# Fewer zero matmuls in front (30 for 43) and six q, k and v loads in flight for four, in a linear-attention and expert-attention kernel

## The chip, the cores and the metric

The kernel runs on one core of one Trainium2 chip. The metric is the device time of one execution in microseconds, lower is better. Three runs of the kernel before are shown.

## The reference

```
kv   = einsum('bhsd,bhse->bhde', k, v)
out  = einsum('bhsd,bhde->bhse', q, kv)
x    = out / sqrt(mean(out^2, -1) + 1e-6) * g_norm   # then heads side by side: (8, 576, 512)
logits = x @ w_gate                                  # top 2 of 4 experts per token, softmax over them
for e in range(4):
    q, k, v = x @ wq[e], x @ wk[e], x @ wv[e]
    a  = causal softmax(q @ k.T / 8)
    ye = a @ v @ wo[e]
    out += weight of e for the token * ye
```

Batch 8, 8 heads, sequence 576, head size 64; four experts with a head of 64 each. q, k and v are float32 in HBM and are read once (9.4 MB each); the result, again 9.4 MB, is written once.

## The kernel before, in words

One core works through eight batches b = 0 to 7. Every piece of work is a task with a name and a batch, and the sequence of all tasks is written out by hand in the string ORDER (lines 30 to 52); `unpack` (line 116) decodes it and the loop at the end of the kernel (lines 840 to 844) emits one task after the other. So each engine executes its instructions in the order in which they come in that string, and a wait at the head of an engine holds everything behind it. The strings ENGINE and SLOTS fix which engine takes a task and which buffer or PSUM bank it uses.

The tasks that the text speaks of:

- `lk`, `lv`, `lq` (lines 332 to 350): loads of half of the k, v or q data of a batch, issued from the SP queue. A batch has four pieces of k, four of v and two of q. k and v have two buffers each.
- `lw` and `ws` (lines 373 to 387): load of half of an expert weight into a stage buffer, and the multiplication by g_norm that puts it into place (on POOL, DVE or ACT).
- `kv` (line 408): for one chunk of two heads, ten matmuls of k with v (line 414). `kvc` and `kvx` copy the result out of PSUM (`kvs`, by ACT or DVE) and, exchanged between groups of 32 partitions, once more (`kvm`, by ACT, DVE or POOL).
- `qc` (line 435): DVE transposes q in blocks (line 437). `o` (line 442) multiplies it with kvs and kvm (line 450).
- `sq`, `ms`, `ln` to `lo`, `bc`, `xm`: squares, sums (line 482), the inverse root, its spreading by matmul (line 563) and the normalised x (line 571, DVE).
- `G` (line 485, the gate's matmuls), `L`, `lt`: the logits of the gate.
- `kp`, `qp`, `v`: projections (lines 643 and 624); `sc`, `exp`, `msk`, `pv`: scores, exponentials, causal mask, weighted sum (lines 674, 686, 693, 719); `y` and `st`: output projection (line 794) and store (line 811).

Batch 0 is split in halves of heads. Its order on the tensor engine is: zero matmuls, `kv` of chunks 2 and 3, zero matmuls, `o` of the second half, zero matmuls, `kv` of chunks 0 and 1, the sums of the second half, zero matmuls, `o` of the first half. On DVE two transposes of q stand ahead of two of the kvm copies that the first `o` reads.

The zero matmuls come from the table ZEROS (line 26): the key is the task ahead of which they stand, the value their number. Each multiplies a 128x128 tile of zeros with itself (line 836) into a part of a bank that the task is about to use and that nothing reads; in float32 each one is two passes, so that 43 of them are 86 passes in the profile. They wait for nothing but the memset of the zeros and whoever holds the bank. No result depends on them.

FLIGHT (line 19) is used in one place:

```
def queued(task, ins):
    if len(task) > 1 and task[0] in ("lk", "lv", "lq") and task[1] > 1:
        tc.add_manual_dep(ins.ins, moved[-FLIGHT].name, order_only, reason="queue")
    moved.append(ins.ins)
```

`moved` is the list of all loads and stores that went through `queued`. A q, k or v load of batch 2 or later waits until the transfer FLIGHT places earlier in that list has landed. Loads of batches 0 and 1, weights and stores carry no such wait. Apart from it, a transfer waits for the semaphore lane that it takes, of which there are eight, and a load for the release of its buffer. The wait stands in the SP queue, so that it also holds what comes behind it there.

Of the kernel before, what the change touches and what calls it, by code (L numbers as in the profile page):

```python
# [15 lines left out]

NB, NCH, EP, NF = 5, 4, 2, 4
RUN, LO = 9, 4
FLIGHT = 4

NQT, BY_PE = 1, (0, 1, 2, 3, 4, 5, 6, 7)

# [1 line left out]


ZEROS = {
    ("kv", 0, 2): 26, ("o", 0, 1): 9, ("kv", 0, 0): 4, ("o", 0, 0): 4,
}

ORDER = (  # L30
# [96 lines left out]
def kernel(  # L127
# [195 lines left out]
# [4 lines that stand above are left out]
# [548 lines left out]
```

## Time and profile before

| | |
|---|---|
| median of 3 runs | 205.02 us (203.74 to 207.45) |
| the profiled execution's own time | 206.06 us |
| its span, first to last instruction | 204.4 us |
| PE busy (matmuls) | 191.1 us, 94% |
| PEld (weight loads) | 155.5 us, 76% |
| DVE, ACT, POOL busy | 135.9, 129.7, 70.6 us |
| read from HBM, written | 30.42 MB, 9.44 MB |

The profile is of one execution. Its times are counted from the first instruction; busy times of matmuls contain modelled ends, and consecutive ones overlap in a row's duration. The chain of work that ended last is followed back from the last instruction; a piece "DMA k_b<-in_k_dram" in it reaches from the issue of a load to its landing. A row of the timeline gives start, duration, engine, line, operation and tiles, and in brackets the idle time before and what ended it.

### The profile page before, as it was taken

Reading aid. Unit: us, or ns where it says so; the run is one execution under the profiler, and the core shown is the slowest. Engines: PE = TensorE matmul, PEld = TensorE weight load, DVE = VectorE, ACT = ScalarE, POOL = GpSimd, SP = SyncE. Lnnn points to the kernel's source line nnn. Section 1 sums busy time; section 2 is a strip of 40 time slices with the busy share of each in tenths; the row PEclk is TensorE's granted clock in tenths of the full one; section 3 lists DMA queues with packets and bytes.
Section 4 is the critical chain, followed back from the end, with each engine's and each line's share of the span. In section 5 each row is a group of like instructions: output and inputs, shape, how many; then the busy total and the mean of one; then the engine's idle time right before and its main releaser. Section 6 shows DMA issues by size and latency. Waiting matters only on the chain.

```text
span 204.4 us, 7128 instructions
## 1 busy us (share of the span) xinstructions
PE 191.1 (94%) x2943; PEld 155.5 (76%) x2960; DVE 135.9 (66%) x336; ACT 129.7 (63%) x240; POOL 70.6 (35%) x185
## 2 busy tenths in 40 slices
PE   7999899999999889999999999999999999999980
PEld 7976575788787568869878697888967878988740
DVE  7046799969446756766695557765877596667640
ACT  2035536749767268963875978887376647567961
POOL 8101354004355131408163552165126224126500
PEclk9999999999999999999999999999999999999999
DMA  4899997898986998785089960100043134026486
GB/s 151 267 363 354 334 226 196 275 343 247 272 275 213 301 291 310 220 281 192 5 238 337 288 236 3 55 3 0 3 154 145 62 114 152 2 89 205 168 326 195
DMA packets 33808, 40.31 MB, mean 197 GB/s; under 512 B 8288, under 2 KB 24944, under 8 KB 33776
## 3 DMA queue, kind: packets, MB, share of 16 engines
q1 hardware_dynamic: 33248, 39.20, 60.6%
q10 hardware_dynamic: 432, 0.66, 0.9%
q8 instruction: 23, 0.38, 0.8%
q14 instruction: 9, 0.07, 0.1%
q0 software_dynamic: 96, 0.01, 0.1%
HBM read 30.42 MB, written 9.44 MB: 195 GB/s over the span
## 4 chain that ended last, share of the span: by engine, by line
PE 63%; DMA 21%; DVE 5%; ACT 5%; issue 3%; ACTq 0%; POOL 0%; DVEq 0%; SPq 0%; POOLq 0%
PE banks L643 10%; PE banks L450 7%; PE banks L674 7%; DMA k_b<-in_k_dram 7%; DMA q_b<-in_q_dram 6%; PE banks L836 6%; PE banks L624 6%; PE banks L414 6%; PE banks L719 6%; PE banks L482 5%; PE banks L794 5%; DMA v_b<-in_v_dram 5%; DMA out_dram<-stage 4%; PE banks L563 2%; PE banks L762 2%
## 5 line engine op out<-in xcount | busy, mean ns | idle before, releaser
L686 ACT ACTIVATE PT<-banks 128x1024 bf16<-128x1024 f32 (+1 forms) x64 | 51.7, 835 | 11.9 <-PE banks L674 10.2
L693 POOL TENSOR_SCALAR_AFFINE_SELECT PT<-PT 128x256 bf16<-128x256 bf16 (+1 forms) x80 | 29.1, 386 | 20.6 <-ACT PT L686 20.3
L437 DVE STREAM_TRANSPOSE qT<-q_b 128x576 f32<-128x576 f32 x32 | 23.7, 758 | 8.5 <-DMA q_b<-in_q_dram 6.2
L571 DVE TENSOR_TENSOR xT<-banks,ob 128x576 fp32r<-128x576 f32 x32 | 23.4, 746 | 4.1 <-PE banks L563 3.8
L624 PE MATMUL banks<-wv_r,xT 128*128 128x256 f32 x160 | 24.5, 291 | 0.0
L643 PE MATMUL banks<-xT,wk_r 128*128 128x288 f32 x128 | 22.3, 307 | 0.1
L624 PEld LDWEIGHTS banks<-wv_r,xT 128*128 128x128 f32 x160 | 21.2, 189 | 1.4 <-DVE wv_r L387 0.2
L643 PE MATMUL banks<-xT,wq_r 128*128 128x288 f32 x128 | 22.1, 305 | 0.1
L414 PE MATMUL banks<-v_b,k_b 128*64 128x64 f32 x640 | 21.3, 224 | 0.9 <-DMA k_b<-in_k_dram 0.5
L414 PEld LDWEIGHTS banks<-v_b,k_b 128*64 128x64 f32 x640 | 19.7, 138 | 3.1 <-issue 0.9
L674 PE MATMUL banks<-qTp,kT 64*128 64x192 f32 (+3 forms) x224 | 21.3, 307 | 0.4 <-DVE xT L571 0.3
L674 PEld LDWEIGHTS banks<-qTp,kT 64*128 64x128 f32 x224 | 15.8, 185 | 6.0 <-issue 2.0
L643 PEld LDWEIGHTS banks<-xT,wk_r 128*128 128x128 f32 x128 | 18.4, 188 | 1.8 <-ACT ob L311 0.5
L643 PEld LDWEIGHTS banks<-xT,wq_r 128*128 128x128 f32 x128 | 18.3, 188 | 1.9 <-DVE kT L312 0.5
L450 PE MATMUL banks<-qT,kvs 32*64 32x288 f32 x256 | 19.0, 410 | 0.4 <-DVE g_den L608 0.3
L719 PEld LDWEIGHTS <-PT 128*128 128x128 bf16 x480 | 15.9, 97 | 4.5 <-issue 1.5
L474 POOL TENSOR_TENSOR sqs<-ob 128x576 f32<-128x576 f32 x14 | 16.1, 1156 | 7.7 <-DVE ob L312 4.9
L719 PE MATMUL banks<-vext,PT 128*128 128x65 bf16 x480 | 17.5, 193 | 1.0 <-issue 1.0
L450 PE MATMUL banks<-qT,kvm 32*64 32x288 f32 x256 | 18.2, 410 | 0.0
L794 PE MATMUL banks<-wo_b,OT 128*128 128x512 bf16 (+1 forms) x57 | 16.5, 372 | 1.8 <-issue 1.0
L311 ACT COPY stage<-banks 128x512 f32<-128x512 f32 x25 | 14.3, 593 | 5.8 <-PE banks L794 3.4
L311 ACT COPY ob<-banks 128x576 f32<-128x576 f32 x19 | 11.8, 637 | 8.2 <-PE banks L450 8.2
(95 smaller groups left out, 305.9 us busy)
## 6 DMA issues: line engine op xcount, KB each, us to landing
q_b<-in_q_dram SPq DMA_DIRECT2D x16, 576.0 KB, 6.2
out_dram<-stage SPq DMA_DIRECT2D x29, 256.0 KB, 2.6
v_b<-in_v_dram SPq DMA_DIRECT2D x16, 320.0 KB, 5.4
k_b<-in_k_dram SPq DMA_DIRECT2D x16, 320.0 KB, 4.8
v_b<-in_v_dram SPq DMA_DIRECT2D x16, 256.0 KB, 5.0
k_b<-in_k_dram SPq DMA_DIRECT2D x16, 256.0 KB, 5.2
out_dram<-stage SPq DMA_DIRECT2D x9, 128.0 KB, 2.4
stage<-in_moe_wk_dram SPq DMA_DIRECT2D x2, 256.0 KB, 7.3
```

What stands on the lines that cost most here:

```text
L311: return nc.scalar.copy(dst, src)
L414: use(nc.tensor.matmul(p_kv[hh * Dh : (hh + 1) * Dh, c, :], lhsT=k_t(b)[:, h, j, :], rhs=v_t(b)[:, h, j, :], start=(j == 0), stop=(j == LO ...
L437: nc.vector.transpose(q_part(b, dh)[:, ms].rearrange("p m (t i) -> p m t i", t=RUN), q_t(b)[:, ms, :, dh * 32 : (dh + 1) * 32],)
L450: use(nc.tensor.matmul(bank(n)[at : at + Dh, 0:HALF], lhsT=(kvs if z == dh else kvm)[b % 2][pp, m], rhs=q_part(b, dh)[pp, m], start=(dh == ...
L571: use(nc.vector.tensor_tensor(out=xTs[b % 2][:, 0 : NCH * S].rearrange("p (n s) -> p n s", s=S)[:, cs, cols], in0=both(ns)[:, :, 0:HALF], ...
L624: use(nc.tensor.matmul(bank(n)[:, at : at + E * Hd], lhsT=blocks_of(xTs[b % 2], c)[:, i * P : (i + 1) * P], rhs=w_r["v"][:, c, :, :].rearr ...
L643: use(nc.tensor.matmul(bank(n)[:, 0:HALF], lhsT=w_r[nm][:, c, 2 * pr : 2 * pr + 2, :].rearrange("p e f -> p (e f)"), rhs=blocks_of(xTs[b % ...
L674: use(nc.tensor.matmul(bank(ns[el])[:, o : o + hi - lo], lhsT=kTs[(2 * b + pr) % 3][pp, kb * P : (kb + 1) * P], rhs=tiles["qTp", b, pr][pp ...
L686: use(nc.scalar.activation(PTs[(2 * b + pr) % 3][:, :, 512 * j : 512 * j + o], both(ns)[:, :, 0:o], ACTF.Exp, scale=scale), *ns)
L693: nc.gpsimd.affine_select(out=d, in_=d, compare_op=AluOpType.is_ge, fill=0.0, base=0, pattern=[[0, 2], [1, w]], channel_multiplier=-1,)
L719: use(nc.tensor.matmul(heads[el][:, k_ * W1 : (k_ + 1) * W1], lhsT=PT[:, el, col : col + P], rhs=vexts[b % 2][:, kb, 2 * pr + el, :], star ...
L794: use(nc.tensor.matmul(bank(n)[:, 0 : cols.stop - cols.start], lhsT=OT[:, pr, at : at + P], rhs=wo_b[:, pr, cols], start=(pr == 0), stop=( ...
```

## The change

Two constants are changed. The four groups of zero matmuls have 20, 6, 2 and 2 members where they had 26, 9, 4 and 4, and FLIGHT is six where it was four.

```
-FLIGHT = 4
+FLIGHT = 6
...
 ZEROS = {
-    ("kv", 0, 2): 26, ("o", 0, 1): 9, ("kv", 0, 0): 4, ("o", 0, 0): 4,
+    ("kv", 0, 2): 20, ("o", 0, 1): 6, ("kv", 0, 0): 2, ("o", 0, 0): 2,
 }
```

Apart from 13 zero matmuls less, the sequence of instructions is the same on all engines and in the SP queue. What differs in the SP queue is which earlier transfer a load waits for.

## The prediction

> **What bounds the kernel now.** I read the page first, then who waited on PE, the chain that ended last, busy time by stretch, and last the single rows of the front.
>
> ```profile
> span 204.4 us, 7128 instructions
> PE 191.1 (94%) x2943; PEld 155.5 (76%) x2960; DVE 135.9 (66%) x336; ACT 129.7 (63%) x240; POOL 70.6 (35%) x185
> ```
>
> ```profile
> PE banks L719 <- issue: 1.0, 1, 1.0
> PE banks L414 <- DMA k_b<-in_k_dram: 0.5, 1, 0.5
> PE banks L414 <- ACT PT L686: 0.4, 1, 0.4
> PE banks L674 <- DVE xT L571: 0.3, 1, 0.3
> ```
>
> PE is busy for 94% of the span and works in a fixed order, so only two things can shorten the run: PE work that goes away, and PE's few waits. (The columns of the second view: us in total, times, longest.) The zeros are PE work that nobody reads. Their place in the chain that ended last, each row with its start and length:
>
> ```profile
> 1.12 8.11 PE banks L836 x52
> 9.23 1.34 PE banks L414 x40
> 10.59 0.28 ACT kvs L311
> 10.91 2.27 PE banks L836 x18
> 13.18 1.16 PE banks L450 x32
> 14.34 1.09 PE banks L836 x8
> 15.43 1.31 PE banks L414 x40
> 16.74 1.09 PE banks L482 x8
> 17.84 1.09 PE banks L836 x8
> 18.93 1.24 PE banks L450 x32
> ```
>
> The second half of the change concerns the loads of batches 2 to 7. The same chain later:
>
> ```profile
> 33.00 4.51 DMA k_b<-in_k_dram
> 37.52 5.19 DMA k_b<-in_k_dram
> ...
> 64.91 3.59 DMA k_b<-in_k_dram
> 68.49 0.14 issue
> 68.63 1.40 PE banks L414 x34
> ```
>
> From 33.00 to 68.49 seven loads follow each other without a gap, each issued as an earlier one lands, and PE's L414 at 68.63 waits for the last. This is the limit of four in flight. Loads in the front, which have no such limit, and loads in the middle (time to landing, shortest, median, longest; after it the DMA share and GB/s, the last two columns, of a stretch of each):
>
> ```profile
> DMA to landing us min/median/max: 7.0/7.7/8.2
> ```
>
> ```profile
> DMA to landing us min/median/max: 3.8/4.8/6.6
> ```
>
> ```profile
> 16.50:23.40 6.90, 5.96 (x84) 3.72 (x80) 4.87 (x12) 4.47 (x10) 0.57 (x2) 1.00 1.12 338
> 43.00:68.60 25.60, 24.03 (x448) 19.96 (x447) 16.52 (x37) 18.06 (x29) 10.07 (x24) 1.00 0.86 267
> ```
>
> A deeper queue makes each load later after its issue (7.7 for 4.8 us) but moves more: 338 for 267 GB/s.
>
> **Part 1, the zeros.** Price of a pass, from the zeros alone (PE busy and count are the first columns after the length):
>
> ```profile
> 1.12:4.97 3.85, 3.85 (x18) 1.00 0.62 188
> 4.97:9.16 4.19, 4.19 (x36) 1.00 0.87 275
> ```
>
> Before 4.97 a pass takes 3.85 / 18 = 0.214 us, after it 4.19 / 34 = 0.123 (two of the 36 began earlier), although the granted clock reads 1.00 in both. The six zeros removed from the first group are 12 passes of the fast kind: 1.48 us, and the first group would end at 9.16 - 1.48 = 7.68. The others: six passes of 2.27 / 18 = 0.126, 0.76 us; twice four of 1.09 / 8 = 0.136, 1.09 us. In all 3.3 us of PE time. What of it arrives depends on what is late next, step by step.
>
> ```profile
> 2.97 0.62 SPq L332 DMA_DIRECT2D k_b<-in_k_dram  x1
> 6.24 1.50 SPq L332 DMA_DIRECT2D k_b<-in_k_dram  x1
> ```
>
> ```profile
> k_b<-in_k_dram SPq DMA_DIRECT2D x1, 256.0 KB, 5.4
> ```
>
> ```profile
> k_b<-in_k_dram SPq DMA_DIRECT2D x1, 256.0 KB, 7.7
> ```
>
> ```profile
> 10.30 1.44 DVE L437 STREAM_TRANSPOSE qT<-q_b 128x576 f32<-128x576 f32 x2 [4.88 <-DMA q_b<-in_q_dram]
> 11.77 0.47 DVE L312 COPY kvm<-kvs 32x128 f32<-32x128 f32 x2
> 15.90 1.44 DVE L437 STREAM_TRANSPOSE qT<-q_b 128x576 f32<-128x576 f32 x2
> 64.91 0.78 DVE L437 STREAM_TRANSPOSE qT<-q_b 128x576 f32<-128x576 f32 x1 [1.31 <-DMA q_b<-in_q_dram]
> ```
>
> The last k piece of the first half lands at 2.97 + 5.4 = 8.4; with the 0.14 us from landing to matmul of the chain's end above, the first kv starts at 8.5: 0.7 earlier, not 1.48. The second group of zeros would end at 11.7; o(0,1) then waits for DVE's kvm copies at 11.77 to 12.24, which stand behind transposes that start with the landing of q: o starts at 12.1 to 12.3, 0.9 earlier. kv(0,0) waits for the k piece that lands at 6.24 + 7.7 = 13.9 and starts at 14.1, 1.3 earlier. The sums follow; then two zeros instead of four, 0.55 less: o(0,0) starts at 17.0, 1.9 earlier. It reads the first of DVE's two transposes at once and the second half way, at 17.6; they are done at 16.6 and 17.34 even if nothing moves them.
>
> From here the gain passes through ACT and DVE. The projections of k wait for a weight that POOL scales:
>
> ```profile
> 23.64 3.19 POOL L387 TENSOR_SCALAR wk_r<-stage,g_part 128x256 fp32r<-128x256 f32 x3 [5.82 <-DMA stage<-in_moe_wk_dram]
> ```
>
> ```profile
> 28.27 1.29 PE L643 MATMUL banks<-xT,wk_r 128*128 128x288 f32 x8
> ```
>
> POOL starts when the weight lands, behind loads that run at full rate, so it ends at 26.83 in both kernels. L643 can't start before 26.9: 1.4 earlier. What follows on DVE waits for neither POOL nor this load, so PE may get a little of the 1.9 back. I take **1.5 us** for this part. Its ends: 0.9 (the gain of the first o, should the sums' chain be held) and 3.3 (all of the zeros' time). I take the value near 1.4 because two landings and the POOL row hold it there.
>
> **Part 2, six in flight.** With 338 for 267 GB/s the stretch from 33.00 to 68.49 would take 35.5 x 267 / 338 = 28.0 us. Six is less deep than the front's queue of up to eight, so the true lead is between nothing and 7.5 us; the front's lead of 1.5 has to be covered, and 2 to 5 us are likely, more than any wait needs. PE then loses the 0.52 us ahead of L414 at 68.63, and the 0.35 ahead of L674: xT stood behind DVE's transpose at 64.91, which waited 1.31 us for q. Of the 0.36 ahead of L414 at 63.49, ACT's exponentials keep most; I count 0.13. Together **1.0 us**; ends 0 (the lead is used up) and 1.2 (all three). No load is put ahead of another in the SP queue, and a load's buffer is still released by PE, now 1.5 us earlier. Behind the load that waits in SP stand other loads and the first two stores; none waits longer than now. Costs: the PE wait of 1.0 at L719 has no data wait behind it and I leave it as it is (rival three).
>
> **Sum.** 1.5 + 1.0 = 2.5 us. Of the profiled execution: 206.06 - 2.5 = 203.6. That execution was 1.04 above the median of the three runs, so on the median: 205.02 - 2.5 = **202.5**, 1.2% faster.
>
> **A rule beside it.** In this trace the pass of the zeros gets short 3.85 us after PE starts. The Trainium skill, "TensorE: Matmul & The Clock Gate", Part 1, says that the tensor clock is doubled only after a busy window of about 3.4 us, and that this window runs freely, so that the same kernel meets it after different numbers of matmuls. By that rule the change would come at 3.4 to 6.8 us of work, the trace's 3.85 being an early draw, and part 1 would be worth more in other executions (rival one). The same page (Why this matters for your kernels) warns of PE idle gaps over about 3 us; the waits that the sum opens in the front are 0.8 us (7.68 to 8.5) and less, so by it nothing is lost; the trace agrees as far as 16.50 to 23.40 goes, 0.94 us idle in 6.90 with passes still short.
>
> **The rivals.** One: the short passes begin later in most executions. If none came inside the zeros, the 12 removed passes cost 12 x 0.214 = 2.6 and the first kv starts that much earlier; all zeros together 4.4 us. With 1.0 of part 2 the bounds are 3.3 + 1.0 and 4.4 + 1.0 (2.6 + 0.76 + 1.09 = 4.4), that is 200.7 to 199.6; I name **200.5**. For it: runs from 203.74 to 207.45 differ by more than the sum. Against: POOL's 26.83 caps the gain as soon as the front is early.
>
> Two: the gain is hidden. The idle time opened in the front slows PE's passes again (18 passes at 0.214 for 0.123: 1.6 us), or the lead is lost at the DVE chain: 0 to -0.9 us, **204.5**. Against: waits of 0.5 us in the front now don't do it.
>
> Three, the other side: PE's instructions come late. The 0.99 us wait at L719 is put to "issue", no landing and no semaphore; PE's program is fetched by the same 16 DMA engines:
>
> ```profile
> q8 instruction: 11, 0.18, 0.8%
> ```
>
> That is the count of 30 to 118 us, where six will be in flight. If each fetch cost PE one such wait: 11 x 0.99 = 10.9 us more, 205.02 - 2.5 + 10.9 = **213.4**. It turns the sum from three such waits on, and it is slower by over 2% from seven. Against: in the front, with more in flight, no PE wait is put to issue. The Trainium skill, "DMA: Bandwidth & Descriptors" (Queues, rings and completion order), says that an engine takes turns between queue rows packet by packet; by it a longer row of loads would hold a fetch no longer than a short one, and no run yet shows it.
>
> **How the numbers follow.** The forecast 0.50, rival one 0.25, two 0.12, three 0.13. Two per cent, 4.1 us, is about what a measurement of this kernel can tell from no change. Rival one lies beyond it on the fast side: faster 0.25. Of rival three 0.11 lies beyond it: slower 0.11; the rest, 0.64, within. The forecast's own range is 200.9 to 204.1 (from the two per cent, where rival one begins, to the parts' lower ends, 0.9 and 0). The range 199.7 to 206.8 takes in rival one, rival two, and rival three up to four waits (202.5 + 4 x 0.99 = 206.5), and leaves out some 0.15.
>
> **What would show it.** In the changed profile the first L414 starts at 8.5, right behind a k landing; L450 at 12.1 to 12.3 and 17.0; L643 at 26.9 behind POOL's wk_r; no L414 waits for DMA near 67; loads take 6 to 7 us to land and 43 to 68 shows over 300 GB/s. It would be wrong if the first L643 starts later than 27.5, if L414 still waits for k_b, or if new PE waits put to issue appear.

## The result and the profile after

The kernel after takes 202.71 us (median of 18 runs, 201.67 to 204.51), the kernel before beside it 205.11 (18 runs, 203.74 to 207.78). The ratio is 0.9913, with a 95% interval from 0.9883 to 0.9942. The profiled execution of after took 203.93 us, its span is 202.2. (Ratios here and below leave out executions that took over 1.5% more than their kernel's fastest; medians have all of them.)

That profiled execution lost part of its clock in the front, and its page shows it. The span, the busy times and the granted clock in 40 slices:

```profile
span 202.2 us, 7076 instructions
PE 188.7 (93%) x2917; PEld 153.2 (76%) x2934; DVE 135.5 (67%) x336; ACT 129.6 (64%) x240; POOL 70.3 (35%) x185
PEclk9969999999999999999999999999999999999996
```

The third slice, 10 to 15 us, has a granted clock of 0.6, all the others but the last 0.9 or more. Who waited on PE, the columns as before:

```profile
PE banks L414 <- DMA k_b<-in_k_dram: 2.5, 1, 2.5
PE banks L563 <- DVE lo L520: 1.3, 2, 1.0
```

One wait for a k piece is left, and it is in the front. The waits at L674 and L719 and the one of L414 near 68 us are gone. The chain of after shows the same:

```profile
2.96 6.80 DMA k_b<-in_k_dram
...
9.90 1.40 PE banks L414 x40
...
11.64 2.93 PE banks L836 x12
14.57 1.21 PE banks L450 x32
15.77 0.64 PE banks L836 x4
16.41 1.31 PE banks L414 x40
...
67.99 1.32 PE banks L414 x40
```

The k piece issued at 2.96 takes 6.8 us to land where it took 5.4 before. PE has finished its zeros by 7.42 and starts the first kv at 9.90. Twelve zero passes then take 2.93 us. The stretches (the columns behind the busy times are granted clock, DMA share and GB/s; in the first two rows the stretch is 3.41 us, one period of the clock, as shown below):

```profile
7.85:11.26 3.41, 1.36 (x40) 1.28 (x40) 0.00 (x0) 0.00 (x0) 0.00 (x0) 1.00 0.95 303
11.26:14.68 3.42, 3.06 (x21) 2.82 (x28) 1.88 (x4) 0.86 (x3) 0.00 (x0) 0.50 1.06 376
...
43.00:67.90 24.90, 24.48 (x454) 20.51 (x454) 16.25 (x38) 17.49 (x29) 9.99 (x24) 1.00 0.94 312
```

PE was idle for 3.41 - 1.36 = 2.05 us of the first stretch, and in the next its clock was 0.50. From 43 to 68 us the loads now move 312 GB/s (267 before).

To compare all kernels I cut PE's time at three points that all of them have: the first matmul of the kv of batch 2, the first L762 (it follows the L719 that waited before), and PE's last matmul. The cuts are starts and ends of PE rows of each trace, in us; the second column is the landing of the last k piece that the first kv needs, which is issued at 2.96 in every kernel.

| profiled kernel | k piece lands | kv of batch 2 starts | from there to L762 | from L762 to PE's end |
|---|---|---|---|---|
| before | 8.37 | 43.38 | 30.97 | 124.56 |
| after | 9.76 | 44.02 | 28.44 | 124.32 |

So in these two executions the front cost 0.64 us more, the middle 2.53 less and the rest 0.24 less; the tail behind PE is 5.44 in both. The sum is 2.13; the spans differ by 2.2 as they are rounded here, by 2.14 unrounded.

### The profile page after: what moved, and what is told of

Same layout as the page of the kernel before. It is cut to its first block, busy times and chain, and to the rows that moved or that the text cites. A ratio compares the mean times of both kernels' runs of the same rounds, so it can differ in the third digit from the quotient of the medians.

```text
span 202.2 us, 7076 instructions
## 1 busy us (share of the span) xinstructions
PE 188.7 (93%) x2917; PEld 153.2 (76%) x2934; DVE 135.5 (67%) x336; ACT 129.6 (64%) x240; POOL 70.3 (35%) x185
## 4 chain that ended last, share of the span: by engine, by line
PE 74%; DVE 8%; ACT 5%; DMA 5%; issue 4%; POOL 1%; SPq 0%; DVEq 0%; ACTq 0%; POOLq 0%
PE banks L643 13%; PE banks L414 9%; PE banks L674 8%; PE banks L450 8%; PE banks L482 8%; PE banks L624 7%; PE banks L719 6%; PE banks L794 6%; DMA k_b<-in_k_dram 3%; PE banks L563 3%; DVE qT L437 3%; PE banks L762 2%; PE banks L836 2%; DMA out_dram<-stage 2%; PE banks L545 1%
## 5 line engine op out<-in xcount | busy, mean ns | idle before, releaser
L414 PE MATMUL banks<-v_b,k_b 128*64 128x64 f32 x640 | 21.1, 224 | 2.5 <-DMA k_b<-in_k_dram 2.5
L414 PEld LDWEIGHTS banks<-v_b,k_b 128*64 128x64 f32 x640 | 19.7, 138 | 4.6 <-issue 3.0
L643 PE MATMUL banks<-xT,wk_r 128*128 128x288 f32 x128 | 22.3, 307 | 0.1
L643 PE MATMUL banks<-xT,wq_r 128*128 128x288 f32 x128 | 22.1, 305 | 0.1
L674 PE MATMUL banks<-qTp,kT 64*128 64x192 f32 (+3 forms) x224 | 21.3, 307 | 0.0
L674 PEld LDWEIGHTS banks<-qTp,kT 64*128 64x128 f32 x224 | 15.8, 185 | 5.5 <-issue 2.0
L643 PEld LDWEIGHTS banks<-xT,wk_r 128*128 128x128 f32 x128 | 18.4, 188 | 1.8 <-ACT ob L311 0.5
L643 PEld LDWEIGHTS banks<-xT,wq_r 128*128 128x128 f32 x128 | 18.2, 188 | 1.9 <-DVE kT L312 0.5
L450 PE MATMUL banks<-qT,kvs 32*64 32x288 f32 x256 | 19.1, 412 | 0.4 <-DVE g_den L608 0.3
L719 PEld LDWEIGHTS <-PT 128*128 128x128 bf16 x480 | 15.8, 97 | 3.4 <-DVE ob L312 0.9
L450 PE MATMUL banks<-qT,kvm 32*64 32x288 f32 x256 | 18.3, 411 | 0.0
L311 ACT COPY stage<-banks 128x512 f32<-128x512 f32 x25 | 14.1, 593 | 5.4 <-PE banks L794 4.1
L719 PE MATMUL banks<-vext,PT 128*128 128x65 bf16 x480 | 17.4, 193 | 0.0
```

The lines of the kernel that those rows point to most:

```text
L311: return nc.scalar.copy(dst, src)
L414: use(nc.tensor.matmul(p_kv[hh * Dh : (hh + 1) * Dh, c, :], lhsT=k_t(b)[:, h, j, :], rhs=v_t(b)[:, h, j, :], start=(j == 0), stop=(j == LO ...
L450: use(nc.tensor.matmul(bank(n)[at : at + Dh, 0:HALF], lhsT=(kvs if z == dh else kvm)[b % 2][pp, m], rhs=q_part(b, dh)[pp, m], start=(dh == ...
L643: use(nc.tensor.matmul(bank(n)[:, 0:HALF], lhsT=w_r[nm][:, c, 2 * pr : 2 * pr + 2, :].rearrange("p e f -> p (e f)"), rhs=blocks_of(xTs[b % ...
L674: use(nc.tensor.matmul(bank(ns[el])[:, o : o + hi - lo], lhsT=kTs[(2 * b + pr) % 3][pp, kb * P : (kb + 1) * P], rhs=tiles["qTp", b, pr][pp ...
L719: use(nc.tensor.matmul(heads[el][:, k_ * W1 : (k_ + 1) * W1], lhsT=PT[:, el, col : col + P], rhs=vexts[b % 2][:, kb, 2 * pr + el, :], star ...
```

## The experiments

The theory after this profile had three parts. The zeros are worth about 1.4 us when the k piece lands as before, and in the profiled execution a late landing and the clock hid that. Six in flight removes the waits for loads near 63 to 69 us. And the wait put to issue at L719 is a packet of PE's instructions that starts late while loads are queued: the theory of the held packet, D where it has a letter. The rivals: the deeper queue alone did it all; the zeros alone did it all; the wait at L719 belongs to its place in the program and has nothing to do with loads.

**One part alone.** The first kernel has the new zeros and four in flight, the second the old zeros and six.

```
 FLIGHT = 4
-    ("kv", 0, 2): 26, ("o", 0, 1): 9, ("kv", 0, 0): 4, ("o", 0, 0): 4,
+    ("kv", 0, 2): 20, ("o", 0, 1): 6, ("kv", 0, 0): 2, ("o", 0, 0): 2,
```

> Theory A (the prediction): fewer zeros are worth 1.5 us by themselves: ratio to the kernel before near 0.993, about 203.6 us, and the first L643 starts near 26.9. Theory B (from the changed kernel's profile, where the first kv waited 2.48 us for a k piece and L643 started 0.6 later than before): the zeros are worth nothing, 0 to +0.6 us, ratio 1.000 to 1.003; with four in flight L414 near 68 still waits for k_b.

Measured: 202.64 us (6 runs) to 205.55 of before; ratio 0.9882 (0.9820 to 0.9944). By the medians that is 2.9 us less, more than either theory expected of the zeros alone.

```
-FLIGHT = 4
+FLIGHT = 6
```

> Theory A: six in flight are worth 1.0 us: ratio 0.995, about 204.1 us. Theory B: they are worth all of the change, 1.8 to 2.4 us, ratio 0.988 to 0.991; both: no L414 waits for DMA after 30 us and 43 to 68 us shows over 300 GB/s.

Measured: 204.22 us (12 runs); ratio 0.9963 (0.9926 to 0.9999).

Both unchanged kernels were profiled once more on the same chip.

> The changed kernel once more, for a second profile. A: the last k piece of the first half lands near 8.4, PE waits under 1 us ahead of the first L414, and the granted clock stays at 1.00 until 20 us. B: the landing is near 9.8 again, PE waits over 2 us there, and the clock falls to 0.50 behind it. If the landing differs between executions of one kernel, the front's share differs with it.

> The kernel before once more, for a second profile: if the front's landings are a matter of the execution, the last k piece lands anywhere from 8.4 to 9.8 us, and with 43 zeros PE's wait ahead of the first L414 stays under 1 us in either case. If the 1.0 us put to issue at L719 is a fixed property of this order with four in flight, it is there again; if it is chance, it is not.

Measured: 201.72 and 207.22 us for one execution each. The rows of the table for these four:

| profiled kernel | k piece lands | kv of batch 2 starts | from there to L762 | from L762 to PE's end |
|---|---|---|---|---|
| zeros alone | 8.71 | 41.94 | 29.50 | 124.38 |
| six in flight alone | 7.32 | 43.11 | 28.10 | 124.59 |
| after, second profile | 8.43 | 42.00 | 28.10 | 124.37 |
| before, second profile | 9.45 | 44.44 | 31.27 | 124.42 |

The front goes with the zeros: where the k piece lands near 8.4 to 8.7 us, kv of batch 2 starts at 41.9 to 42.0 with 30 zeros and at 43.4 with 43. The middle goes with the queue: 28.1 with six, 29.5 to 31.3 with four. In the zeros alone the rows of PE and POOL show both halves (two places of the timeline; POOL is GpSimd):

```profile
25.36 1.91 POOL L387 TENSOR_SCALAR wk_r<-stage,g_part 64x256 fp32r<-64x256 f32 x2
...
27.32 0.79 PE L643 MATMUL banks<-xT,wk_r 128*128 128x288 f32 x4 [0.26 <-POOL wk_r L387]
```

```profile
67.07 1.39 PE L414 MATMUL banks<-v_b,k_b 128*64 128x64 f32 x40 [1.02 <-DMA k_b<-in_k_dram]
```

L643 now waits for the weight that POOL scales, which starts at 25.36 in this kernel and ends at 27.27: the step that the prediction took as the cap. And PE, early by 1.4 us, waits 1.02 us for the k piece: with four in flight the loads did not follow here.

**The wait at L719.** In the second profile of before the wait was longer:

```profile
PE banks L719 <- issue: 1.8, 1, 1.8
PE banks L414 <- DMA k_b<-in_k_dram: 1.1, 1, 1.1
```

PE's instructions come in 23 packets of 16 KB in every kernel, about one for each 256 of PE's matmuls and weight loads (5954 of them in before). The DMA queues of this profile from 69.3 to 71.9 and from 71.9 to 73.9 us (packets, MB, share):

```profile
q1 hardware_dynamic: 317, 0.63, 83.4%
```

```profile
q1 hardware_dynamic: 450, 0.55, 92.5%
q8 instruction: 1, 0.02, 3.0%
```

Its packet starts at 73.25 and PE goes on at 75.67. In before it starts at 71.96 and PE goes on at 74.32. In after it starts at 69.17 and no PE instruction waits. So where PE waits, it goes on 2.4 us after the start of the packet. To try whether the queued loads hold it, one kernel is the kernel before with only two transfers in flight for the seven places in the list of transfers that lie around it:

```
     if len(task) > 1 and task[0] in ("lk", "lv", "lq") and task[1] > 1:
         tc.add_manual_dep(ins.ins, moved[-FLIGHT].name, order_only, reason="queue")
+        if 54 <= len(moved) <= 60:
+            tc.add_manual_dep(ins.ins, moved[-2].name, order_only, reason="queue")
```

> The kernel before, 43 zeros and four in flight, but seven transfers (the two of wo, q of batch 4 and what follows of batch 5) wait until only two are in flight; so the queue is short near 69 us. Theory D (the 1.0 to 1.8 us that PE waits at L719 are an instruction packet that stands behind loads): the packet of that place starts 1 us or more earlier than near 72, the wait put to issue at L719 is gone, and the time is 0.7 to 1.8 us shorter, although fewer loads are in flight. Against D (the wait has to do with the order of PE's work or with data): the wait stays, and the time is the same or longer.

Measured: 210.17 us, ratio 1.0175 (1.0116 to 1.0233). The packet starts at 70.16, with two loads in flight, 1.8 and 3.1 us earlier than in the two profiles of before, where four are, although PE is no further on than there (kv of batch 2 starts at 44.24). The middle takes 28.35 us. Of the wait 0.25 us is left: the last matmul of that L719, at 72.55, comes 2.39 us after the packet's start and 0.28 behind the matmul before it, where the others follow at 0.03. So, as far as one profile against two can show it, the length of this wait hangs on when the packet starts, and the packet starts earlier with fewer loads in flight. The 0.7 to 1.8 us that were expected of it did not come. The time went elsewhere (who waited on PE, the lines numbered two higher; then two stretches):

```profile
PE banks L645 <- DVE root L516: 3.8, 1, 3.8
PE banks L416 <- DMA k_b<-in_k_dram: 1.4, 1, 1.4
```

```profile
82.73:86.15 3.42, 0.51 (x4) 0.51 (x4) 1.65 (x4) 0.29 (x1) 0.00 (x0) 1.00 0.86 285
86.15:89.56 3.41, 3.17 (x12) 2.35 (x12) 2.42 (x8) 1.66 (x4) 2.24 (x5) 0.50 0.92 283
```

A q load now lands late, DVE's transpose behind it too, PE is idle for 3.8 us, and the clock is 0.50 for the next 3.41. From L762 to PE's end it takes 129.76 us for 124.4.

The place of the wait is set by the program. The waits of this kind in all profiles, counted in PE's matmuls and weight loads, stand behind the 2241st (both profiles of before), the 1729th (eight in flight and 12 in the first group, below) and the 2752nd (six in flight alone again, below): multiples of 256 apart, to within one, as the packets are. Thirteen zeros less are 52 such instructions less (26 matmul passes and as many weight loads), so with 30 zeros the 2241st is no longer at L719 but within L643. PE reaches it 4.2 to 6.2 us after the packet's start, with four in flight (4.2 and 4.3 in the two profiles of the zeros alone) as with six or eight, so no wait shows. With 43 zeros and six in flight it is still at L719; there the packet starts at 67.9 with three loads in flight, PE comes 3.1 and 3.2 us later and does not wait. Either part of the change is enough to end this wait.

**After again, 26 zeros in the first group, eight in flight.** These three ran on one chip.

> The changed kernel beside the three others of this call: ratio to the kernel before near 0.99. Executions whose mean granted clock is 0.990 or less, which lost the clock behind the first group of zeros, should be some one in five and lie 1.5 to 2 us above the others.

```
-    ("kv", 0, 2): 20,
+    ("kv", 0, 2): 26,
```

> The changed kernel with 26 zeros again in the first group (6, 2 and 2 in the others). Theory A (the first group's zeros are late work: less of them is earlier): the same as the changed kernel or up to 0.7 us slower. Theory C (from 20 zeros on, the first kv waits for its k piece anyway, and what the last six do is to keep PE busy until it lands): no slower, up to 0.4 us faster in the median, PE's wait ahead of the first L414 under 1 us, no granted clock of 0.50 between 10 and 190 us in any profile, and no execution with a mean clock of 0.990 or less.

```
-FLIGHT = 6
+FLIGHT = 8
```

> The changed kernel with eight in flight. A: nothing is left for it to remove, no L414 waits for DMA after 30 us already with six: same time as with six within 0.5 us, and 43 to 68 us at 312 GB/s or a little more. Rival three of the prediction (PE's instructions come late behind a longer queue): instruction packets start later, PE waits put to issue of 1 us or more appear in 30 to 118 us, and the time is 1 to 3 us longer.

Measured, to 206.5 us of before: 202.81 (ratio 0.9833, 0.9778 to 0.9887), 202.77 (0.9811, 0.9756 to 0.9867) and 202.37 (0.9809, 0.9761 to 0.9857). No two of them can be told apart. Neither the six zeros of the first group nor a still deeper queue is a term that this measurement sees. The mean clock was 0.990 or less in three of the six executions of after, where one in five was expected, and in none of the six of each of the others. In eight in flight one PE wait put to issue appears in another place, L414 at 61.80, 0.9 us, 2.6 us after its packet's start at 59.18.

**Fewer zeros, and the parts once more.** Four kernels on one chip. The first makes PE idle longer ahead of the first kv, to test the clock.

```
-    ("kv", 0, 2): 20,
+    ("kv", 0, 2): 12,
```

> The kernel after with 12 zero matmuls in the first group instead of 20: 24 passes, which end near 5.7 us, while the k piece lands at 8.3 to 9.8, so that PE idles 2.6 to 4.1 us. The theory (an idle stretch of 2.5 us and more costs the granted clock of a 3.41 us period, and the zeros are there to prevent it) expects a granted clock of 0.50 in the records of 8 to 15 us, a mean clock of 0.990 or less in nearly all executions, the second group of 12 passes at over 0.2 us each, and 0.6 to 2 us more than the kernel after beside it. Against it (the zeros of the first group are free time, since kv waits for the k piece in both): the same time as after within 0.3 us.

Measured: 204.17 us (12 runs), beside 202.79 of after on this chip: 1.4 us more at the median. The ratio to before, from six of the twelve executions, is 0.9910 (0.9862 to 0.9957), the same as after's. The mean clock was 0.990 or less in 10 of 12 executions, and 0.974 to 0.982 in the six slowest. In its profile, the two stretches of 3.41 us from 5.21:

```profile
5.21:8.62 3.41, 1.50 (x31) 1.34 (x32) 0.20 (x3) 0.00 (x0) 0.91 (x2) 1.00 0.89 266
8.62:12.04 3.42, 3.06 (x33) 2.88 (x29) 1.56 (x3) 0.86 (x3) 0.00 (x0) 0.50 0.92 300
```

1.91 us idle, although the k piece landed at 7.78, the earliest but one; the clock fell as expected. The theory of the clock holds, though less idle time was enough than the 2.5 us that it named.

> The 30 zeros with four in flight, beside the other two on one chip. The theory (the two parts act at different places, only the wait at L719 is counted in both) expects 1.5 to 2.9 us less than before, and 0.3 to 1.3 us more than the whole change, with a wait of L414 for a k piece near 67 us. Against it (the deeper queue adds nothing once the front is early): the same time as the whole change within 0.3 us.

> 43 zeros with six in flight. The theory expects 0.6 to 1.5 us less than before, no wait of L414 for a k piece near 67 us and none at L719 put to issue. Against it (the queue changes no time by itself): the time of before within 0.3 us.

> The whole change once more, on the same chip as its two parts. The theory expects 2.3 to 3.5 us less than before, and no more than the sum of the two separate gains. Against it (the parts get into each other's way): no less time than the better of the two parts alone.

Measured, to 205.0 us of before (29 runs): zeros alone 203.84 (10 runs; ratio 0.9914, 0.9869 to 0.9958), six in flight alone 204.09 (12 runs; 0.9958, 0.9928 to 0.9989), both 202.79 (8 runs; 0.9910, 0.9876 to 0.9944). By the medians the parts add: 1.16 + 0.91 = 2.07 to 2.21 of the whole. By the ratios (seven of the ten executions of the zeros alone) the queue adds nothing to the zeros; the intervals don't decide it. Against the expectation, L414 near 68 us waited for less than 0.2 us in this profile of the zeros alone. The rows of the table for these kernels and for the three of the group before:

| profiled kernel | k piece lands | kv of batch 2 starts | from there to L762 | from L762 to PE's end |
|---|---|---|---|---|
| zeros alone, again | 9.76 | 44.11 | 28.20 | 124.83 |
| six in flight alone, again | 8.04 | 43.01 | 28.12 | 125.78 |
| after, third profile | 8.25 | 41.82 | 28.12 | 124.35 |
| after, fourth profile | 9.23 | 42.46 | 28.44 | 124.35 |
| 26 in the first group | 9.81 | 43.16 | 28.11 | 125.05 |
| eight in flight | 8.09 | 41.83 | 29.25 | 124.39 |
| 12 in the first group | 7.78 | 42.20 | 29.90 | 124.34 |

The zeros alone had a late front here (late landing, clock at 0.50 from 11.16 to 14.57, as in the first profile of after), and its loads then kept up: 28.20. With an early front they did not: 29.50. But a late front does not decide it: with 43 zeros kv of batch 2 starts as late, and four in flight took 30.97 and 31.27 there (0.99 and 1.81 of them the wait at L719), six 28.10 and 28.12. With four in flight L414 near 68 us waits 0.52 and 1.09 us in the profiles of before, 1.02 and 0.19 in those of the zeros alone, and not at all in two in flight at one place; with six or eight it waits in none of nine profiles. So the deeper queue takes away a wait that comes in some executions, with 43 zeros as with 30. What sets it in one execution and not in the next stays open. The two longer middles with six or eight in flight each hold one late packet; for 12 in the first group:

```profile
PE banks L414 <- DMA k_b<-in_k_dram: 1.9, 1, 1.9
PE banks L414 <- issue: 1.5, 1, 1.5
```

This packet starts at 60.82, with six loads in flight, and PE goes on at 63.27. The second profile of six in flight alone has one too (0.88 us at 89.52), behind L762, which is 0.88 of the 1.4 us by which its last column is long; the rest of that column was not traced.

## Why the prediction was right, and where it was not

The total was right: 202.71 measured, 202.5 predicted, and for the profiled execution 203.93 to 203.6. Its terms were not all right; in the profiled pair two errors offset each other.

**Part 1, taken as 1.5 us.** The mechanism and the size hold when the k piece lands as in the trace of before. (By the medians the zeros alone gained 2.9 us on one chip and 1.2 on another, on either side of 1.5.) The second profile of after goes through the predicted steps (first kv, second kv, the first half's L450, L643):

```profile
8.56 1.39 PE L414 MATMUL banks<-v_b,k_b 128*64 128x64 f32 x40 [0.32 <-DMA k_b<-in_k_dram]
...
14.12 1.39 PE L414 MATMUL banks<-v_b,k_b 128*64 128x64 f32 x40
...
27.20 0.80 PE L643 MATMUL banks<-xT,wk_r 128*128 128x288 f32 x4 [0.17 <-POOL wk_r L387]
```

Predicted were 8.5, 14.1 and 26.9 (one matmul of L643 goes ahead at 26.66). The first o starts between 11.99 and 12.24 (12.1 to 12.3), the second at 17.2 (17.0). Kv of batch 2 is 1.4 us early.

**The step that failed** is "the waits that the sum opens in the front are 0.8 us (7.68 to 8.5) and less, so by it nothing is lost". It took one landing, 8.37, for the landing. Over 14 profiled executions the same load, issued at the same time, lands between 7.32 and 9.88. In the first profile of after it landed at 9.76, the wait was 2.48 us, the clock fell, and L643 started at 28.88 where the prediction had named 27.5 as the sign that it is wrong. The 43 zeros, 26 of them in the first group, covered most of these landings (the latest, 9.88, still made PE wait 1.36 us); 20 in the first group do not. How often it costs the clock can be estimated from the mean clock of an execution: the four profiled ones with a drop have 0.983 to 0.987, the ten without 0.992 to 0.999. A mean of 0.990 or less have 13 of the 55 runs with 30 zeros, 10 of the 12 with 12 in the first group, and none of the 24 with 43 zeros and six in flight. Of the 57 runs of before beside the experiments, with 43 zeros and four in flight, six have it, all of them at 206.6 us or more; none of these was profiled, so where they lost the clock is open. In the 18 runs of after the four such runs are the four slowest, 203.93 to 204.51.

The rule cited beside it, from the Trainium skill, "TensorE: Matmul & The Clock Gate" (Why this matters for your kernels), warns of idle gaps over about 3 us. Here a gap of 1.91 us was enough, so that the measurement decides against it. Its other rule (Part 1), a window of some 3.4 us that runs freely, agrees: the records change in steps of 3.41 us, at another phase in each execution.

**Part 2, taken as 1.0 us.** Right: six in flight alone gained 1.3 and 0.9 us by the medians of two chips. L414 no longer waits near 68, L674 no longer for xT, and the 0.36 us at 63.49, of which 0.13 was counted, is gone as a whole in after. From kv of batch 2 to the L414 near 68 it took 25.25 us (43.38 to 68.63) before and 23.90 (44.02 to 67.92, where its first row starts) after: 1.35 us, to 1.23 for all three waits. The rate, 312 GB/s, lies over the 300 named. The whole middle is 2.9 to 3.2 us shorter in the profiles of six in flight alone than in those of before, more than these medians gain; but the profiled executions of before were 0.95 and 1.67 us slower than the medians beside them, and the first of six in flight alone 1.67 faster.

**The wait at L719, left as it is.** Wrong: it went with the change, 0.99 us in the profiled pair and 1.81 against the second profile of before. The zeros alone are enough for it, since they move the place where PE needs the packet, and the deeper queue alone too, since the packet starts earlier. In the profiled execution the end of this wait offsets what the late landing took from part 1. That its total came out so close, 203.93 for 203.6, was luck. How much of this wait a median execution of before has is not known; both profiled ones were slower than the median.

**The rivals.** One: the short passes do begin late, but at 3.95 to 6.95 us after the first instruction over 14 profiles. It moves the end of the zeros, and the k piece sets the start of kv anyway; 202.71 is not 200.5. Two: "the idle time opened in the front slows PE's passes again" does happen, in about a quarter of the executions, not in most. Three: the late packet is real and acts on both sides. With six or eight in flight it cost 0.9 to 1.5 us once in three of nine profiles, not eleven times in each; with four in flight and 43 zeros it cost 1.0 and 1.8 in both, with four and 30 zeros nothing of this size in two. The page cited, "DMA: Bandwidth & Descriptors" of the Trainium skill (Queues, rings and completion order), by which a longer row of loads would hold a fetch no longer than a short one, is not borne out as far as this goes: with two loads for four the packet came earlier, in one profile. What in the engines holds it stays open.

## What to carry to other kernels

Filler work ahead of a load must be sized for the load's late landings, not for the one in the profile; profile several executions before shaving it. When a front is made earlier, ask at once whether the loads behind it can follow: a part of the gain can be given back at the next wait for data. A deeper queue took such waits away here, with the early front and without it. A wait that the profile puts to issue need not be a constant of the program: look for the instruction packet behind it, for the loads in flight beside it, and for what the change does to the count of instructions ahead of it.

## What the runs showed of the hardware that was not expected

The clock falls for a whole period of 3.41 us after a period in which PE was idle for about half. PE's idle time in the period ahead, from busy rows of stretches as above: 1.91, 2.05, 2.14 and 2.91 us ahead of the four drops (12 in the first group, after, zeros alone again, two in flight at one place). The largest without a drop are 1.55 and 1.51 (after's fourth profile and zeros alone), the next 1.47. The ends of the executions agree: of the periods in which PE stops, one with 1.95 us idle is followed by a drop (after's third profile), one with 1.55 is not (before's second). The fourth profile of after, the period and the one behind it:

```profile
8.18:11.60 3.42, 1.87 (x44) 1.77 (x45) 0.90 (x2) 0.75 (x3) 0.00 (x0) 1.00 0.90 305
11.60:15.01 3.41, 3.28 (x58) 2.40 (x59) 1.35 (x4) 1.15 (x3) 0.00 (x0) 1.00 1.07 365
```

So the limit lies between 1.55 and 1.91 us of 3.41 in these traces. All four drops had their idle time in one gap, while the 1.55 and 1.51 were made of two, of 1.2 us and 0.4; so whether it is the sum or the longest gap that counts is not shown.

PE goes on 2.4 to 2.6 us after the start of the late packet in all five waits of this kind (2.36, 2.42, 2.45, 2.48 and 2.62 us, in before, its second profile, 12 in the first group, six in flight alone again and eight in flight). Each had three to seven loads in flight when the packet started. All five stand a multiple of 256 matmuls and weight loads apart, to within one.
